# Batch-0 sink shares over all 128 partitions, constant rows as planned loads, loads without hold-back, and a new written-out order

## The chip, the cores and the metric

The kernel runs on one core of one Trainium2 chip. The metric is the device time of one execution in microseconds. It is compared as the median over runs. The profile shows five engines: PE (matmul; PEld is its weight load), DVE (vector), ACT (scalar), POOL (GpSimd) and SP, which here only issues DMAs. ACT and POOL issue DMAs as well, from the same instruction queue in which their other work stands.

## The reference

The program is an attention layer with sink tokens and a sliding window, followed by a ResMLP block. The sizes are 4 batches, 8 heads, 768 tokens, 64 values per head, so 512 values per token, and 2048 in the hidden layer.

```python
scores = scale * np.matmul(q, k.transpose(0, 1, 3, 2))
keep = (pos[None, :] < 4) | ((rel >= 0) & (rel < 128))      # 4 sink tokens, window of 128
a = softmax(np.where(keep, scores, -1e9))
x = np.matmul(a, v)  # -> [4, 768, 512]

a1 = alpha1 * x + beta1
tok = np.einsum('ts,bsd->btd', w_tok, a1)
u = x + lam * tok
a2 = alpha2 * u + beta2
ch = np.maximum(a2 @ w_ch1, 0.0) @ w_ch2
return u + lam * ch
```

## The kernel before

**Plan and order.** The kernel first lists tasks. Each task names its engine choices, what it needs and which buffers it uses (`add`). Four tables written out by hand then fix everything: `ORDER` is the sequence of the tasks, `ENGINES` the engine of each, `HOMES` the buffer of each tile, and `IDLES` where PE gets idle matmuls on a tile of zeros. `emit` walks through `ORDER`. Costs, due times (`lands`) and earliest times (`since`) that stand at the tasks do nothing when the kernel runs: they are what the tables were once planned from. Within one engine the instructions run in the order of the table.

**Batch 0.** Six q/k tiles of head pairs 1 to 3 are loaded by POOL with a cast to 16 bits (`n`); the two of head pair 0 are loaded by SP and cast on DVE. `trans` transposes them on PE (`tp`), and ACT or DVE copies them to `qkT`. `scores_by_pair` and `scores` make the scores of a block of 128 keys (S, in two PSUM buffers), and ACT takes the exponential (E). `sinks` does the same for the four sink tokens (`sk`, `es`): the score rows of two heads each lie at 32 partitions, so heads 0 to 3 (group G = 0) take partitions 0 to 63 and heads 4 to 7 (G = 1) partitions 64 to 127. `pv` multiplies E by v; from the third block of rows on it begins with the sink shares. DVE divides by the sum (`rec`, `x`), POOL multiplies by lam * alpha1 (`xh`).

**MLP.** `wtok` blocks are cast with their row sums, transposed and copied to `wtokT`. `tok` multiplies them with the xh of all six row blocks. `beta` and `ua` finish u on DVE, ACT or POOL cast it (`u16`), PE transposes it (`uTp`), and `mlp1` multiplies it with `w1f` (h). `w1f` arrives in four slices of 512 columns, loaded by POOL with a cast; h number fi needs slice fi // 4. Batch 0 ends with plain products (`mlp2`, ch). Batches 1 to 3 use half-size products of sums (`prod`, P). The attention of batch b + 1 is mixed into the MLP of batch b.

**Queues.** A DMA instruction waits in its engine's queue for what its buffer needs, and for the landing of an earlier DMA whose semaphore it uses again: SP and ACT share eight of these in turn, POOL has eight. Before the change, all twelve v loads of batch 0 (`load_v0`) are issued by SP. Three `gate` loads of a few bytes from w1f stand in SP's queue. Each waits until its w1f slice has landed, and the loads of batch 1 and of w2 are listed with such a gate's slice as a need.

**Constant rows.** lam, alpha1 and beta1 are each loaded to four partitions, and alpha2 and beta2 to `ab_row`, by five loads that ACT issues ahead of the planned order. `fold_rows` makes lam * alpha1 and lam * beta1 from them.

Of the kernel before, what the change touches and what calls it, by code (L numbers as in the profile page):

```python
# [77 lines left out]
def kernel(  # L78
# [17 lines left out]
    nc = tc.nc  # L96
# [45 lines left out]
        "nat": 8, "vnat": 4, "n16": 4, "qkT": 1, "E": 6, "es": 1, "x": 12, "xh": 6,  # L142
# [26 lines left out]
    nc.scalar.dma_start(ab_row[0:NC], moe_alpha2.rearrange("(c p) -> c p", p=P))  # L169
    nc.scalar.dma_start(ab_row[NC : 2 * NC], moe_beta2.rearrange("(c p) -> c p", p=P))  # L170
# [20 lines left out]
    for o_, src in ((lam_r, moe_lam), (la1_b, moe_alpha1), (lb1_b, moe_beta1)):  # L191
        nc.scalar.dma_start(
            o_.rearrange("(a i) d -> a i d", i=32)[:, 0, :], src.unsqueeze(0).to_broadcast([4, DM]))
# [4 lines left out]
    for r in range(NR):  # L198
# [13 lines left out]
    ROWS = 7000.0  # L212
# [4 lines left out]
        26, 6, 9, 7, 10, 5, 11, 8, 18, 15, 72, 19, 1, 12, 3, 0, 4, 2, 22, 14, 73, 74, 45, 48, 46,  # L217
        17, 39, 49, 47, 53, 13, 40, 50, 41, 90, 95, 43, 91, 51, 54, 103, 52, 16, 44, 61, 104, 42,
        96, 109, 100, 62, 107, 110, 63, 55, 28, 108, 92, 56, 101, 21, 68, 65, 59, 93, 20, 69, 97,
        102, 111, 94, 24, 98, 57, 60, 30, 112, 105, 23, 58, 99, 113, 128, 106, 114, 116, 25, 131,  # L220
        135, 78, 115, 64, 27, 138, 31, 32, 117, 132, 29, 129, 136, 33, 122, 66, 125, 34, 123, 137,
        119, 139, 126, 35, 79, 70, 120, 140, 124, 84, 71, 80, 133, 130, 141, 67, 146, 85, 134, 121,
        147, 144, 75, 118, 158, 86, 154, 148, 159, 145, 142, 87, 149, 150, 155, 160, 143, 76, 88,
        151, 156, 81, 77, 166, 152, 162, 167, 89, 127, 82, 163, 213, 83, 168, 209, 164, 165, 214,
        210, 153, 217, 179, 211, 178, 157, 197, 229, 36, 212, 215, 218, 185, 216, 226, 230, 219,
        176, 161, 177, 220, 169, 223, 222, 232, 225, 224, 221, 227, 237, 233, 279, 238, 234, 228,
        273, 280, 182, 171, 204, 291, 274, 175, 289, 292, 200, 231, 293, 290, 246, 294, 295, 199,
        384, 241, 248, 188, 186, 257, 296, 247, 172, 243, 277, 174, 181, 242, 259, 258, 187, 170,
        278, 267, 37, 260, 271, 358, 268, 198, 285, 349, 272, 381, 301, 286, 366, 351, 303, 302,
        189, 297, 378, 173, 304, 281, 180, 352, 203, 249, 190, 282, 298, 379, 250, 287, 380, 192,  # L230
        353, 385, 288, 206, 283, 386, 369, 375, 367, 265, 284, 368, 202, 370, 266, 363, 376, 371,
        253, 377, 201, 299, 254, 372, 364, 183, 382, 191, 300, 373, 615, 365, 275, 374, 383, 357,
        261, 276, 408, 262, 387, 263, 184, 409, 205, 195, 239, 411, 264, 410, 395, 269, 396, 240,
        397, 270, 196, 388, 614, 621, 235, 412, 400, 194, 244, 398, 236, 401, 255, 617, 251, 245,
        256, 389, 390, 399, 252, 311, 359, 207, 193, 391, 424, 616, 335, 425, 393, 341, 426, 392,
        336, 648, 427, 634, 413, 394, 312, 636, 414, 428, 419, 404, 420, 415, 360, 405, 313, 429,
        208, 422, 337, 416, 361, 441, 421, 622, 402, 314, 423, 442, 626, 403, 305, 638, 315, 406,
        430, 640, 316, 435, 431, 306, 641, 355, 436, 443, 619, 437, 338, 649, 618, 438, 362, 317,
        432, 637, 407, 307, 433, 345, 444, 339, 439, 635, 318, 445, 450, 434, 639, 644, 319, 451,
        628, 452, 620, 440, 308, 645, 340, 453, 417, 446, 323, 447, 418, 320, 309, 448, 324, 321,  # L240
        658, 322, 329, 449, 642, 659, 454, 325, 625, 643, 330, 646, 347, 455, 326, 623, 343, 647,
        464, 344, 456, 465, 348, 466, 460, 457, 467, 650, 327, 458, 331, 461, 629, 459, 472, 462,
        632, 463, 653, 356, 651, 656, 627, 332, 38, 654, 480, 333, 342, 624, 652, 473, 310, 476,
        468, 471, 470, 469, 481, 474, 488, 885, 477, 475, 482, 492, 655, 490, 493, 350, 483, 478,
        514, 491, 516, 489, 657, 479, 515, 660, 517, 630, 882, 665, 518, 663, 354, 328, 666, 502,
        880, 661, 664, 498, 879, 519, 508, 499, 346, 503, 678, 662, 512, 509, 679, 504, 513, 487,
        484, 671, 485, 676, 486, 506, 677, 877, 548, 505, 672, 680, 507, 526, 549, 546, 527, 631,
        334, 522, 674, 681, 528, 547, 907, 523, 534, 903, 529, 633, 682, 675, 878, 542, 683, 535,
        890, 689, 543, 550, 685, 684, 690, 510, 551, 494, 511, 673, 667, 544, 495, 668, 891, 496,
        686, 545, 901, 687, 669, 497, 693, 888, 688, 883, 530, 694, 670, 700, 531, 524, 897, 701,  # L250
        698, 500, 691, 525, 696, 699, 552, 501, 697, 704, 553, 558, 695, 705, 904, 692, 562, 559,
        706, 909, 887, 707, 563, 564, 898, 708, 702, 566, 565, 910, 715, 703, 567, 532, 716, 889,
        713, 533, 709, 714, 896, 520, 710, 556, 717, 521, 538, 557, 537, 540, 539, 536, 560, 541,
        899, 718, 921, 572, 922, 881, 711, 574, 884, 573, 576, 712, 561, 719, 902, 577, 575, 555,
        727, 720, 569, 908, 721, 580, 728, 578, 722, 581, 729, 554, 723, 905, 730, 568, 739, 724,
        579, 725, 592, 570, 911, 726, 582, 740, 593, 588, 912, 583, 595, 584, 571, 906, 743, 589,
        731, 585, 900, 590, 732, 605, 744, 587, 733, 596, 606, 734, 607, 611, 594, 597, 602, 745,
        612, 586, 613, 599, 895, 603, 591, 757, 765, 600, 758, 601, 759, 766, 741, 771, 760, 742,
        916, 772, 751, 917, 746, 773, 752, 913, 761, 919, 774, 886, 767, 918, 604, 762, 763, 598,
        768, 777, 764, 779, 920, 923, 780, 914, 755, 915, 778, 608, 756, 926, 930, 735, 609, 931,  # L260
        924, 927, 781, 736, 925, 775, 782, 737, 928, 753, 929, 893, 738, 934, 754, 892, 769, 935,
        932, 610, 941, 770, 819, 776, 942, 894, 939, 820, 821, 940, 937, 936, 823, 749, 822, 945,
        748, 824, 938, 747, 827, 933, 948, 950, 750, 952, 943, 951, 825, 953, 787, 828, 944, 807,
        788, 797, 826, 808, 949, 946, 829, 798, 801, 954, 830, 791, 802, 956, 947, 792, 783, 955,
        957, 963, 961, 784, 789, 958, 962, 811, 790, 964, 959, 785, 812, 965, 805, 786, 795, 806,
        960, 967, 796, 799, 793, 968, 966, 970, 972, 794, 813, 971, 969, 815, 973, 814, 809, 800,
        816, 803, 810, 974, 978, 804, 976, 979, 837, 975, 977, 835, 838, 980, 841, 836, 839, 842,
        818, 843, 840, 845, 981, 832, 982, 846, 817, 986, 844, 831, 990, 987, 983, 988, 847, 991,
        984, 851, 833, 992, 1002, 993, 834, 848, 855, 852, 985, 849, 1003, 859, 856, 1004, 989,
        1006, 850, 860, 1005, 853, 998, 1007, 1008, 868, 999, 857, 1009, 997, 865, 995, 858, 862,  # L270
        996, 869, 866, 1000, 874, 994, 854, 1001, 1016, 863, 875, 1040, 1017, 1038, 1041, 1032,
        1039, 871, 1020, 872, 1028, 1021, 1011, 1024, 1029, 1013, 1018, 1033, 1012, 1025, 1034,
        1019, 1036, 1010, 1035, 1042, 1037, 1076, 1043, 1070, 1077, 870, 1074, 1071, 1054, 1075,
        1022, 1055, 1060, 1023, 1048, 1061, 1058, 1049, 1066, 1059, 1014, 1044, 1015, 1067, 1072,
        1045, 1056, 1073, 1026, 1057, 1078, 1068, 1079, 1064, 1069, 1046, 1027, 1050, 1063, 1047,
        1052, 1082, 1053, 1051, 1084, 1083, 1062, 1065, 1030, 1085, 1080, 1101, 1031, 1081, 1091,
        1102, 1107, 1092, 1097, 1093, 1103, 864, 1108, 1105, 867, 1098, 1111, 1106, 1104, 1113,
        1112, 1089, 1114, 1115, 1086, 1116, 1090, 861, 1094, 1087, 1117, 1099, 1109, 1100, 1121,
        1095, 1110, 1125, 1118, 1122, 1124, 1134, 1126, 1123, 1128, 1135, 1127, 1119, 1136, 1088,
        1140, 1120, 873, 876, 1131, 1129, 1141, 1096, 1137, 1142, 1132, 1130, 1133, 1138, 1139,  # L280
    )
    ENGINES = (
# [22 lines left out]
        "1202002102135312330203"  # L305
    )
    IDLES = (
        (73, 0, 65), (46, 0, 12), (49, 1, 1), (90, 3, 10), (61, 3, 2), (109, 3, 3), (92, 3, 1),
        (166, 1, 4), (162, 0, 1),
    )  # L310
    W1_SINCE = 20000.0
# [3 lines left out]
    XB = 2  # L315
# [1007 lines left out]
```

The softmax here doesn't subtract the row's maximum and nothing guards it: scores larger than these inputs give would overflow.

## Time and profile before

| What | us |
|---|---|
| median of 3 runs | 258.96 (258.18 to 259.81) |
| profiled execution, span | 254.3 |
| PE busy / DVE / ACT / POOL | 245.6 / 190.7 / 133.2 / 103.2 |
| last PE matmul ends, last instruction of the chain on DVE | 250.06, 250.08 |
| first ACT copy | 8.13 |
| first scores of batch 0 on PE | 11.19 |
| first xh on POOL | 20.27 |
| idle matmuls on PE in the first 31 us | 99 in nine stretches |

The span runs from the first to the last instruction of the profiled execution. The median is of runs that are timed as a whole, so it is longer by what lies around the span. The granted TensorE clock is 0.997 of full speed. PE's busy time counts the idle matmuls too, and the ends of matmuls are modelled, so a busy PE in the first 31 us does not mean useful work. DMA is busy in the whole first half: its share in the 40 slices of the page is 0.6 or more up to slice 19. In what follows, L711 and the like are lines of the kernel before.

### The profile page before, as it was taken

To read this page: it belongs to the slowest core of one execution; us is meant where nothing else is said; L and a number is where in the kernel's file an instruction comes from. 1 tells how busy PE (TensorE), PEld (TensorE's weight loads), DVE (VectorE), ACT (ScalarE), POOL (GpSimd) and SP (SyncE) were. 2 spreads that over 40 slices of the span, in tenths; PEclk is the share of its full clock that TensorE was granted. 3 is DMA by queue.
4 is the path that set the end of the run, shared out by engine and by line. 5 is a ranking of instruction groups with operands and counts; after the bars stand their busy time and mean duration, and the time that the engine had idled before them with its cause. 6 is when DMAs were issued, how large, how long until landed. Compare 5 with 4: busy or idle time off the path is not lost.

```text
span 254.3 us, 5499 instructions
## 1 busy us (share of the span) xinstructions
PE 245.6 (97%) x2167; PEld 159.9 (63%) x2167; DVE 190.7 (75%) x402; ACT 133.2 (52%) x219; POOL 103.2 (41%) x124
## 2 busy tenths in 40 slices
PE   7799997999999999999999999999999999999993
PEld 7554644666555544566687686667667676667882
DVE  5688986767888874978879995578778983228892
ACT  2599913879977034787833434566660235543000
POOL 8318845876455527515782040065662120000010
PEclk9999999999999999999999999999999999999998
DMA  6999999899999999998484764520000140100327
GB/s 182 205 215 266 272 269 316 246 377 300 221 158 233 234 208 156 195 249 180 110 170 107 128 122 138 144 65 0 3 0 3 30 84 13 41 0 3 117 73 268
DMA packets 86129, 38.79 MB, mean 153 GB/s; under 512 B 73540, under 2 KB 80460, under 8 KB 86104
## 3 DMA queue, kind: packets, MB, share of 16 engines
q1 hardware_dynamic: 66576, 28.06, 47.3%
q10 hardware_dynamic: 15784, 7.11, 11.8%
q0 software_dynamic: 3744, 3.28, 8.0%
q8 instruction: 17, 0.28, 0.4%
q14 instruction: 8, 0.07, 0.1%
HBM read 29.91 MB, written 6.29 MB: 142 GB/s over the span
## 4 chain that ended last, share of the span: by engine, by line
PE 84%; DMA 11%; DVE 2%; POOL 1%; SPq 0%; issue 0%
PE h L929 32%; PE P L1046 22%; PE tok L849 9%; PE ch L1114 8%; DMA w1f<-in_moe_w_ch_dram 8%; PE pv L718 3%; PE S L617 3%; DMA nat<-in_k_dram 3%; PE tp L507 1%; POOL w1f L448 1%; PE tp L504 1%; DVE qkT L157 1%; DVE E L696 1%; PE pv L711 1%; PE pv L604 1%; PE idle L148 0%
## 5 line engine op out<-in xcount | busy, mean ns | idle before, releaser
L929 PE MATMUL h<-uT,w1f 128*128 128x384 f16 x512 | 89.8, 326 | 1.5 <-DMA w1f<-in_moe_w_ch_dram 1.5
L929 PEld LDWEIGHTS <-w1f 128*128 128x128 f16 x512 | 48.2, 98 | 32.7 <-DMA w1f<-in_moe_w_ch_dram 1.9
L935 ACT ACTIVATE hT<-h 128x384 f16<-128x384 f32 x77 | 37.0, 491 | 39.5 <-PE h L929 39.3
L937 DVE TENSOR_SCALAR hT<-h 128x384 f16<-128x384 f32 x51 | 27.8, 555 | 23.4 <-PE h L929 22.8
L1046 PEld LDWEIGHTS <-hT 128*128 128x128 f16 x408 | 39.5, 98 | 6.7 <-issue 0.2
L639 ACT ACTIVATE E<-S 128x1024 f16<-128x1024 f32 (+1 forms) x39 | 38.1, 1001 | 7.6 <-PE S L617 6.3
L762 POOL TENSOR_TENSOR tm<-x,la_b 128x512 f32<-128x512 f32 x18 | 24.3, 1353 | 24.2 <-DVE x L744 12.3
L849 PE MATMUL tok<-xh,wtokT 128*128 128x512 f16 x144 | 33.0, 379 | 0.0
L1059 DVE TENSOR_TENSOR x<-x,P 128x256 f32<-128x256 f32 x45 | 18.3, 419 | 11.3 <-PE P L1046 10.2
L1046 PE MATMUL P<-w2f,hT 128*128 128x256 f16 x216 | 26.5, 273 | 0.0
L849 PEld LDWEIGHTS <-wtokT 128*128 128x128 f16 x144 | 13.9, 98 | 15.0
L1114 PE MATMUL ch<-w2f,hT 128*128 128x512 f16 x96 | 23.2, 379 | 0.0
L1046 PE MATMUL P<-w2s,hT 128*128 128x256 f16 x192 | 23.1, 273 | 0.0
L1082 POOL TENSOR_TENSOR x<-x,pt 128x256 f32<-128x256 f32 x4 | 3.4, 854 | 47.5 <-DVE pt L1077 47.5
L155 ACT CAST u<-x 128x512 f16<-128x512 f32 x15 | 9.2, 615 | 24.9 <-DVE x L856 24.3
L744 DVE TENSOR_TENSOR x<-pv,rec 128x256 f32<-128x256 f32 x48 | 20.4, 425 | 1.7
L155 ACT CAST n<-nat 128x768 f16<-128x768 f32 x21 | 16.9, 828 | 8.9 <-DVE x L1125 6.4
L718 PEld LDWEIGHTS <-E 128*128 128x128 f16 x328 | 14.8, 98 | 5.1 <-issue 1.1
L856 DVE TENSOR_TENSOR x<-x,tok 128x512 f32<-128x512 f32 x24 | 16.0, 683 | 2.3 <-PE tok L849 2.3
L718 PE MATMUL pv<-vfs,E 128*128 128x65 f16 x328 | 17.7, 194 | 0.0
L579 POOL TENSOR_SCALAR_AFFINE_SELECT E<-E 128x512 f16<-128x512 f16 x12 | 7.5, 648 | 20.6 <-ACT E L639 20.6
L743 DVE RECIPROCAL rec<-pv 128x4 f32<-128x4 f32 x48 | 8.6, 179 | 7.2 <-PE pv L718 6.9
(134 smaller groups left out, 340.6 us busy)
## 6 DMA issues: line engine op xcount, KB each, us to landing
wst_w<-in_moe_w_ch_dram SPq DMA_DIRECT2D x8, 512.0 KB, 8.2
nat<-in_q_dram SPq DMA_DIRECT2D x10, 384.0 KB, 3.9
vnat<-in_v_dram SPq DMA_DIRECT2D x14, 256.0 KB, 5.7
nat<-in_k_dram SPq DMA_DIRECT2D x8, 384.0 KB, 7.2
out_dram<-x SPq DMA_DIRECT2D x11, 256.0 KB, 3.1
out_dram<-x ACTq DMA_DIRECT2D x10, 256.0 KB, 3.7
wtn<-in_moe_w_tok_dram SPq DMA_DIRECT2D x6, 384.0 KB, 4.1
w1f<-in_moe_w_ch_dram POOLq DMA_DIRECT2D x4, 512.0 KB, 15.4
```

Of the source, the lines that this page charges most:

```text
L155: nc.scalar.copy(o, i)
L639: nc.scalar.activation(eT.t, pS.t[:, :, 0 : n * w].rearrange("p e (i w) -> p e i w", i=n), AF.Exp, scale=scale)
L718: nc.tensor.matmul(po.t[:, hl, :], eT.t[:, e_, off + i, c : c + P], vf[j][:, h, :], start=(r < 2 and n == 0), stop=(n == len(parts) - 1 an ...
L744: nc.vector.tensor_mul(bx.t[:, 4 * G : 4 * G + 4, :], po.t[:, :, 0:D], rec.t.to_broadcast([P, 4, D]))
L762: engine[e].tensor_mul(bt.t, bx.t.rearrange("p h d -> p (h d)"), la1_b)
L849: nc.tensor.matmul(pt.t, wtokT[:, si, ti * P : (ti + 1) * P], hs[si].t, start=(si == 0), stop=(si == NR - 1))
L929: nc.tensor.matmul(ph.t, w1f[:, c, fi * P : (fi + 1) * P], bu.t[:, c, chk * NTOK : (chk + 1) * NTOK], start=(c == 0), stop=(c == NC - 1))
L935: nc.scalar.activation(bh.t[:, fi, :], ph.t, AF.Relu)
L937: nc.vector.tensor_scalar_max(bh.t[:, fi, :], ph.t, 0.0)
L1046: nc.tensor.matmul(pc.t, hh[:, nt * P : (nt + 1) * P], w(fi), start=(first and n_ == 0), stop=(n_ == HF - 1), skip_group_check=True)
L1059: nc.vector.tensor_add(row(bx)[:, cols], row(bx)[:, cols], pc.t)
L1114: nc.tensor.matmul(pc.t, bh.t[:, fi, nt * P : (nt + 1) * P], w2f[:, fi, :], start=(fi == 0), stop=(fi == NF - 1))
```

## The change

- The sink shares of batch 0 get one buffer for each group (`es`, two homes instead of one). The half of the partitions that belongs to the other group is set to zero by a new step on POOL or DVE, and `pv` multiplies over all 128 partitions instead of 64.
- The five row loads become planned tasks: lam and beta1 stay with ACT, alpha1, alpha2 and beta2 go to SP. The steps that use them list them as needs.
- v loads of batch 0 may be issued by ACT as well.
- The needs that held back loads of batch 1, 2 and 3, and of w2, and the transposes of batch 1, are taken away, and the loads list only their buffers. The three gate loads stay. The tasks for the loads of batch 1 and w2 are listed earlier (`load_rest`).
- ORDER, ENGINES, HOMES and IDLES are replaced as a whole.

```diff
-        "nat": 8, "vnat": 4, "n16": 4, "qkT": 1, "E": 6, "es": 1, "x": 12, "xh": 6,
+        "nat": 8, "vnat": 4, "n16": 4, "qkT": 1, "E": 6, "es": 2, "x": 12, "xh": 6,
...
-    nc.scalar.dma_start(ab_row[0:NC], moe_alpha2.rearrange("(c p) -> c p", p=P))
-    nc.scalar.dma_start(ab_row[NC : 2 * NC], moe_beta2.rearrange("(c p) -> c p", p=P))
...
-    for o_, src in ((lam_r, moe_lam), (la1_b, moe_alpha1), (lb1_b, moe_beta1)):
-        nc.scalar.dma_start(
-            o_.rearrange("(a i) d -> a i d", i=32)[:, 0, :], src.unsqueeze(0).to_broadcast([4, DM]))
...
     IDLES = (
-        (73, 0, 65), (46, 0, 12), (49, 1, 1), (90, 3, 10), (61, 3, 2), (109, 3, 3), (92, 3, 1),
-        (166, 1, 4), (162, 0, 1),
+        (54, 0, 45), (51, 1, 9), (109, 2, 24), (78, 0, 17), (58, 0, 5), (60, 2, 7),
     )
...
-    def load_qk(p, b, hp, t, wait=None):
+    def load_qk(p, b, hp, t):
...
-                p, {SP: 480, ACT: 550}, lambda e: queue[e].dma_start(bf.t, src), [wait], [bf], lands=(16, {(0, 0, 1): 85, (0, 1, 0): 140}.get((b, hp, t), 68)))
+                p, {SP: 480, ACT: 550}, lambda e: queue[e].dma_start(bf.t, src), uses=[bf], lands=(16, {(0, 0, 1): 85, (0, 1, 0): 140}.get((b, hp, t), 68)))
...
-            p, {SP: 520}, lambda e: nc.sync.dma_start(
+            p, {SP: 520, ACT: 560}, lambda e: queue[e].dma_start(
                 bf.t[:, sl], v[0, 4 * G : 4 * G + 4, r * P : (r + 1) * P, :].rearrange("h p d -> p h d")),
...
-        a = add(p, {PE: 336}, tr, [a, wait, done["iden"]], [bn, pt], mode="col" if direct else None)
+        a = add(p, {PE: 336}, tr, [a, done["iden"]], [bn, pt], mode="col" if direct else None)
...
-        if b not in es:
-            es[b] = Buf("es", None, None, f"es{b}")
-        o = qkT[b]
+        if b == 0:
+            es[b, Gs[0]] = Buf("es", None, None, f"es{b}_{Gs[0]}")
+        else:
+            es[b, 0] = es[b, 1] = Buf("es", None, None, f"es{b}")
+        o, eb = qkT[b], es[b, Gs[0]]
...
+        zero = None
+        if n == 1:
+            og = slice(64 - 64 * Gs[0], 128 - 64 * Gs[0])
+            zero = add(p - 1000, {DVE: 160, POOL: 300}, lambda e: engine[e].memset(eb.t[og], 0.0), uses=[eb], port=True)
...
-                g = slice(64 * G, 64 * G + 64) if b == 0 else slice(0, P)
                 nc.tensor.matmul(
-                    po.t, es[b].t[g, (r - 2) * P : (r - 1) * P], vs[g, 4 * G : 4 * G + 4, :],
+                    po.t, es[b, G].t[:, (r - 2) * P : (r - 1) * P], vs[:, 4 * G : 4 * G + 4, :],
                     start=True, stop=False)
...
+        rows = {}
+        for name, o_, src in (("lam", lam_r, moe_lam), ("a1", la1_b, moe_alpha1), ("b1", lb1_b, moe_beta1)):
+            rows[name] = done["row", name] = add(-990, {SP: 500, ACT: 510}, lambda e, o_=o_, src=src: queue[e].dma_start(
+                o_.rearrange("(a i) d -> a i d", i=32)[:, 0, :], src.unsqueeze(0).to_broadcast([4, DM])),
+                lands=(2, 45))
...
+    def load_rest():
+        for i, (hp, t) in enumerate(QK_ORDER):
+            load_qk(t0 + 100 + i, 1, hp, t)
...
```

The new order, where it differs in the first 50 us, engine by engine:

- SP: k and q of head pair 0, a w_tok block, a v tile, the alpha1 row, five v tiles, a w_tok block, two v tiles, then beta2, w_tok, v, alpha2, v and two w_tok blocks; three q/k tiles of batch 1; the first gate; the other loads.
- ACT: the rows of lam and beta1; copies, a w_tok cast and exponentials of head pairs 0 and 1; a v load; five exponentials and a copy; a v load; an exponential; a w_tok load; the rest of group 1.
- POOL: zeroing of one `es` half, the first q load of head pair 1, the identity, the masks, the other five q/k loads, two v casts with lam * alpha1 between them, a third v cast, the first two w1f slices, all twelve xh, the third slice, a u cast, the fourth slice.
- PE: all six tok products ahead of the first uTp (before: five of them), three transposes of batch 1 ahead of the first h, and h in another order.

## The prediction

> **What bounds the kernel now.** I read the chain of waits first, then the timeline of PE, then ACT, POOL and the SP queue in the first 45 us. The chain (start, length, engine, what):
>
> ```profile
> 21.01 2.22 POOL w1f L448 x3
> 23.23 20.17 DMA w1f<-in_moe_w_ch_dram
> ...
> 43.45 2.12 PE h L929 x12
> ...
> 233.45 16.61 PE P L1046 x152
> ```
>
> From 43.45 to 250.06 the chain has PE alone: 206.6 us without a gap above 0.1 us. Its work is the same in both kernels, so the time is decided by when that solid stretch begins. The timeline of PE before it (start, length, operation; in brackets the idle time and its releaser):
>
> ```profile
> 31.39 6.64 PE L849 MATMUL tok<-xh,wtokT 128*128 128x512 f16 x30
> ...
> 39.83 2.11 PE L929 MATMUL h<-uT,w1f 128*128 128x384 f16 x12
> ...
> 43.45 2.12 PE L929 MATMUL h<-uT,w1f 128*128 128x384 f16 x12 [1.50 <-DMA w1f<-in_moe_w_ch_dram]
> ```
>
> PE is solid from 31.39 on but for 1.50 us, in which it waits for the fourth slice of w1f. So before, h begins in effect at 39.83 + 1.50 = 41.33. What sets 31.39? The timeline of ACT:
>
> ```profile
> 23.31 1.02 ACT L639 ACTIVATE E<-S 128x1024 f16<-128x1024 f32 x1
> 24.23 0.83 ACT L814 ACTIVATE wt<-wtn 128x768 f16<-128x768 f32 x1
> ...
> 28.86 1.05 ACT L639 ACTIVATE E<-S 128x1024 f16<-128x1024 f32 x1
> ...
> 30.59 0.83 ACT L155 COPY wtokT<-wT 128x768 f16<-128x768 f16 x1
> ```
>
> ACT has only 0.4 us of idle time between 16.3 and 31.4, and the copy that ends at 31.42 releases tok. ACT bounds the head of the kernel. POOL and SP in the same time, and then how long the v loads of batch 0 take:
>
> ```profile
> 2.24 11.45 SPq L424 DMA_DIRECT2D v<-in_v_dram  x7
> ...
> 13.73 2.71 SPq L435 DMA_DIRECT2D wtn<-in_moe_w_tok_dram  x1
> ...
> 16.49 1.53 SPq L424 DMA_DIRECT2D v<-in_v_dram  x3
> ...
> 20.96 3.05 POOL L448 DMA_DIRECT2D w1f<-in_moe_w_ch_dram  x4
> ...
> DMA to landing us min/median/max: 4.8/9.0/10.2
> ```
>
> SP needs 11.45 us to issue seven v loads. In the program each hardware load waits, in its issuing engine's queue, for the load eight before it. Today that wait stands in SP's queue, where nobody computes.
>
> **The new wait.** In the new order three loads of batch 0 stand in ACT's queue: a v tile after the exponentials of head pair 1, a second v tile, and a w_tok block. The first waits for the landing of the v load that is 14th in SP's queue (v0_0, rows 4), eighth among the v loads. Queued behind it on ACT are five exponentials of group 0, the copy of the last k transposes and all of group 1; PE's scores wait for the two S buffers that these free, DVE and POOL for pv.
>
> When does ACT get there? Its k tile of head pair 1 is now POOL's second casting load, behind the identity (0.2 + 0.3 us in its rows) and five mask steps (1.4), so it is issued near 4.3, where the first is issued at 1.3 as before and takes 0.9. The n loads took 6.7 to 8.3 us to land, so it lands at 11 to 12.6. Transposes, copy and exponentials of the pair (some 4 us) bring ACT to its load at 15 to 16. That the tiles of head pair 0 are now first in SP's queue moves the first scores ahead of 11.19, but the pair behind them does not follow.
>
> When is it released? The eighth v load was issued at 16.49 today, behind the same three big tiles, seven v tiles and one w_tok block; the smallest landing time gives 21.3. If SP were not held up in issuing (the previous issue began at 13.73) it would be 18.5. I take 20.5, nearer to the row in the same place of the queue. So ACT stands still for some 5 us.
>
> What follows on ACT up to the last exponential of group 1, by start to start in the timeline: five of 512 columns at 0.5 = 2.5, seven of 1024 at 0.92 = 6.4, a copy 0.7, two v casts 1.3, one w_tok cast 0.8: 11.7 us. The issue itself is 0.4. Waits for scores were 0.4 in all in this stretch today; with PE held back at the S buffers they can be 2; I take 1.5. Sum: 20.5 + 0.4 + 11.7 + 1.5 = 34.1, and 0.7 for the transposes and the pv behind: tok begins at 34.8 instead of 31.39.
>
> POOL is a second path to the same point. The v tile loaded by ACT lands 4.8 later, at 25.7; its cast (0.8) now stands ahead of the first two w1f issues (1.6) and of all twelve xh products (0.70 to 0.78 each). Nine of them are needed for the first tok: 25.7 + 0.8 + 1.6 + 6.6 = 34.7. The two paths agree.
>
> From tok to h, PE now has 36 tok matmuls at 0.22 (7.9), two w_tok transposes (0.7), two u transposes (0.7) and three transposes of batch 1 moved ahead (1.0; taken off the later stretch): 10.2. First h: 45.0. Against before: 45.0 - 1.0 - 41.33 = +2.7.
>
> **The w1f slices.** Slices 0 and 1 are issued near 27, and with landings of 9.6 to 14.2 (the median of the four was 15.4) they are there by 41. Slice 2 follows the twelfth xh (37), slice 3 the u cast behind tok, three beta rows and a w_tok cast on DVE (41). The lowest landing in the trace is 9.6, the highest 20.2 with four in flight. At 9.6 they land at 46.6 and 50.6; h wants them at 47.0 and 49.6, so the last is 1.0 late. With fewer in flight it can be less: I add 0.5 and keep 0 and 11 (at 20.2) as ends. The 1.50 us stall of today is already out of the sum.
>
> **The other edits.** The sink shares: eight pv of batch 0 go from 64 to 128 rows. Timeline of PE, a pair in each form:
>
> ```profile
> 22.51 0.28 PE L711 MATMUL pv<-vs,es 64*128 64x260 f16 x1
> 22.73 0.41 PE L718 MATMUL pv<-vfs,E 128*128 128x65 f16 x8
> ...
> 70.30 0.27 PE L711 MATMUL pv<-vs,es 128*128 128x260 f16 x1
> 70.41 0.41 PE L718 MATMUL pv<-vfs,E 128*128 128x65 f16 x8
> ```
>
> The next matmul starts 0.22 us after the half-height one and 0.11 after the full one: 8 x 0.11 = 0.9 us of PE. I count it at nothing, for PE fills gaps with idle matmuls there (nine stretches, 99 in all) and ACT is late; without that cover it would be a gain of 0.9. The two zeroings cost 0.2 to 0.5 on POOL, ahead of its first load, and 0.1 to 0.2 on DVE, both before ACT's wait: nothing. The constant rows leave ACT's first 4 us, when it computes nothing (its first copy is at 8.13), and two small ones stand in SP's queue; la is wanted by the first xh, long after: nothing, 0.5 if SP is late by one issue each. The freed loads: three q/k tiles of batch 1 (1.2 MB) now go ahead of the gate in SP's queue, where two w2 blocks and lam_b (1.3 MB) went at 26 to 27; the rest still stand behind that gate. Nothing, since DMA is full either way (share 0.97 to 1.24 from 20 to 46 us); one tile's landing of 5.5 us is the most that could reach PE. Solid stretch and tail: another order of equal work, more v loads in ACT's queue (bounds -0.5 to +2): 0.
>
> Sum: +2.7 + 0.5 = +3.2 on a span of 254.3 and the 4.7 us between span and median: 258.96 + 3.2 = 262.1.
>
> The Trainium skill, "DMA: Bandwidth & Descriptors", section "Issuing engines are not separate DMA queues", speaks against the move of loads to ACT: it says that this saves only the sequencer's issue time. No row here shows a v load issued from ACT; by the rule the transfers gain nothing, and the sum stays as it is.
>
> The same page, "Anatomy of one DMA", puts a DMA at 2.0 us plus its bytes at 436 GB/s, an estimate of 2.3 us for a v tile. The landings of 4.8 to 10.2 us differ from it; by the page's figure ACT would be released at 18.8 and the sum would be 260.4.
>
> **Rivals.** First, the wait is short: SP issues earlier, as ACT has taken loads off it, and ACT goes on at 17. Then the v tile from ACT lands in the crowd, in the median 9.0 us: at 26, and POOL's path (9.0 us of work behind it) puts tok at 35.0 again; in the least, 4.8, at 30.8. The middle, 32.9, is +0.8, or 259.8. The 11.45 us of SP's issue row speak against it.
>
> Second, faster: the early scores pull everything ahead and ACT's v load lands within 4.8 us of 15.5. Then casts, w1f and nine xh end at 29.3, tok begins at 29, h at 39.2: 39.2 - 1.0 - 41.33 = -3.1, 255.8. It decides if the eighth v load has landed when ACT reaches its own. For it: the stall of 1.50 is gone. Against: 16.49 + 4.8.
>
> Third, worse: the last w1f slice, issued late and alone with batch 1's loads, takes 14 us and more. It lands at 55, PE waits 5: 267. For it: landings of 15.4 and 20.2; against: these had four in flight.
>
> **How the numbers follow.** Forecast 0.50 (260.5 to 264.5), short wait 0.22, faster 0.15, late slice 0.13. A difference of 1%, 2.6 us, is about what a measurement of this kernel can tell from none. Slower than 261.55: 0.40 of the forecast, the late slice, 0.03 of the short wait: 0.56. Faster than 256.4: 0.13. The rest, 0.31, lies between. The range of 257.5 to 266 leaves out most of the faster case and half of the late slice. The forecast's own range is 260.5 to 264.5.
>
> **What would show it.** ACT idle for 3 us or more between 15 and 21 before an exponential, released by a v load; tok starting near 35; the first two w1f issues at 26 to 28; first h near 45; PE solid behind it for about 206 us. I am wrong if ACT has no such gap, or if tok starts before 31.4, or if PE has new gaps behind 50 us.

## The result and the profile after

The kernel after takes 272.37 us in the median (271.93 to 272.92, 4 runs), the kernel before 258.57 in the same comparison (255.47 to 259.81). The ratio is 1.0584, with a 95% interval of 1.0504 to 1.0665. The prediction was 262.1, with a range up to 266.0: slower as forecast, but by 13.8 us instead of 3.2.

The profiled execution has a span of 271.2 us against 254.3. I split these 16.9 us at the first h, with the stall of 1.50 us that before has behind it counted to the head:

| Stretch | before | after | difference |
|---|---|---|---|
| start to first h | 41.33 | 51.77 | +10.44 |
| first h to the end of the last P | 208.73 (to 250.06) | 216.07 (to 267.84) | +7.34 |
| tail | 4.24 | 3.36 | -0.88 |

In the later runs, which list time and span of the same execution, the two lie 1.7 to 2.4 us apart, and not the 4.7 us of the prediction. So the profiled execution of before, at 256 to 257, was one of its shorter ones, and the medians differ by less than the spans. Some executions of a kernel are disturbed (over 1.5% above its fastest, most of them at a lower clock): medians and ratios below are of the others, and for two kernels (before_three_u and new_head_old_rest) too few others were left for a ratio, so that the range is given and the profile is of a disturbed one.

The timeline of ACT (start, length, operation; in brackets the idle time and its releaser) shows the predicted wait, and then a second one:

```profile
19.30 0.41 ACTq L422 DMA_DIRECT2D v<-in_v_dram  x1
19.76 0.60 ACT L643 ACTIVATE E<-S 128x512 f16<-128x512 f32 x1 [4.34 <-DMA v<-in_v_dram]
...
24.96 0.39 ACTq L422 DMA_DIRECT2D v<-in_v_dram  x1
...
35.03 0.84 ACT L155 CAST vfs<-v 128x768 f16<-128x768 f32 x1 [3.34 <-DMA v<-in_v_dram]
```

ACT stands still for 4.34 us until it has issued its first v tile. At 24.96 it issues the second, and the cast of that same tile starts 10.07 us later, after ACT has stood still for 3.34 us. The chain of waits has the tile by name, and the SP queue shows what was issued just ahead of it, three tiles of batch 1 of 384 KB each:

```profile
24.96 10.05 DMA v<-in_v_dram
```

```profile
23.42 0.38 SPq L395 DMA_DIRECT2D nat<-in_q_dram  x1
23.90 0.93 SPq L395 DMA_DIRECT2D nat<-in_k_dram  x2
38.11 0.73 SPq L453 DMA_DIRECT2D gates<-w1f  x1
```

PE answers with two gaps. tok begins 8.4 us later than before, and h 10.4 us later than it did in effect:

```profile
20.41 1.01 PE L616 MATMUL S<-biasn,iden 128*128 128x512 f16 x2 [3.97 <-ACT E L643]
...
35.92 0.54 PE L721 MATMUL pv<-vfs,E 128*128 128x65 f16 x7 [3.15 <-ACT vfs L155]
...
39.82 2.93 PE L852 MATMUL tok<-xh,wtokT 128*128 128x512 f16 x8
...
51.77 2.76 PE L932 MATMUL h<-uT,w1f 128*128 128x384 f16 x16
```

Behind the first h, where before has no gap above 0.1 us but the stall of 1.50, PE waits for DVE. These are the five longest of its waits from 60 to 265 us (total, times, longest):

```profile
PE P L1049 <- DVE x L747: 1.5, 1, 1.5
PE h L932 <- DVE x L859: 1.4, 1, 1.4
PE P L1049 <- DVE x L1062: 0.8, 1, 0.8
PE pv L721 <- DVE x L747: 0.7, 1, 0.7
PE P L1049 <- DVE vs L575: 0.5, 1, 0.5
```

All eight add up to 5.7 of the 7.34 us. The rest, and the 1.0 us that the three transposes moved ahead of h should have saved, lies in small delays between matmuls that no run here takes apart.

DVE's busy time went from 190.7 to 207.2 us, in 421 instructions instead of 402. Part of this is dearer instructions, not more of them: the six sums hS took 6.4 us before and take 8.6. Here they are in before and then in after (min/median/max in ns, start of the first and the last):

```profile
L987 DVE TENSOR_TENSOR hS<-hT,hT x6: 944/953/1768, 132.9 to 232.2; 128x1536 f16<-128x1536 f16 x6
```

```profile
L990 DVE TENSOR_TENSOR hS<-hT,hT x6: 948/1429/2026, 147.5 to 247.6; 128x1536 f16<-128x1536 f16 x6
```

### The profile page after: what moved, and what is told of

Read it like the earlier page. It is cut to its first block, busy times and chain, and to the rows that moved or that the text cites. A ratio compares the mean times of both kernels' runs of the same rounds, so it can differ in the third digit from the quotient of the medians.

```text
span 271.2 us, 5544 instructions
## 1 busy us (share of the span) xinstructions
PE 252.3 (93%) x2175; PEld 163.7 (60%) x2175; DVE 207.2 (76%) x421; ACT 125.5 (46%) x201; POOL 105.3 (39%) x129
## 4 chain that ended last, share of the span: by engine, by line
PE 56%; DVE 24%; DMA 10%; issue 4%; POOL 2%; ACT 1%; SPq 1%; ACTq 0%; DVEq 0%; POOLq 0%
PE h L932 22%; PE P L1049 18%; PE tok L852 7%; DMA v<-in_v_dram 6%; DVE w2f L834 4%; PE pv L721 3%; DVE hT L940 2%; DMA lam_r<-in_moe_lam_dram 2%; DVE x L777 2%; DVE E L658 2%; DVE hS L990 2%; PE ch L1117 2%; POOL tm L765 1%; DVE x L747 1%; PE S L621 1%
## 5 line engine op out<-in xcount | busy, mean ns | idle before, releaser
L932 PE MATMUL h<-uT,w1f 128*128 128x384 f16 x512 | 90.8, 326 | 2.0 <-DVE x L859 1.4
L938 ACT ACTIVATE hT<-h 128x384 f16<-128x384 f32 x68 | 32.3, 490 | 43.9 <-PE h L932 43.3
L940 DVE TENSOR_SCALAR hT<-h 128x384 f16<-128x384 f32 x60 | 32.4, 553 | 18.3 <-PE h L932 17.2
L852 PE MATMUL tok<-xh,wtokT 128*128 128x512 f16 x144 | 34.0, 387 | 0.3 <-DVE x L1128 0.3
L583 POOL TENSOR_SCALAR_AFFINE_SELECT E<-E 128x512 f16<-128x512 f16 x20 | 13.8, 713 | 32.2 <-ACT E L643 32.2
L721 PE MATMUL pv<-vfs,E 128*128 128x65 f16 x328 | 18.6, 198 | 4.1 <-ACT vfs L155 3.2
L721 PEld LDWEIGHTS <-E 128*128 128x128 f16 x328 | 16.3, 101 | 9.5 <-issue 4.3
L1088 POOL TENSOR_TENSOR x<-x,pt 128x512 f32<-128x512 f32 x4 | 5.9, 1475 | 41.6 <-issue 32.4
L747 DVE TENSOR_TENSOR x<-pv,rec 128x256 f32<-128x256 f32 x48 | 20.4, 425 | 1.7
L157 POOL CAST u<-x 128x512 f16<-128x512 f32 x9 | 6.0, 662 | 31.4 <-DVE x L859 27.6
L155 ACT CAST n<-nat 128x768 f16<-128x768 f32 x17 | 13.6, 831 | 4.2 <-DMA qkT<-n 3.2
```

The lines of the kernel that those rows point to most:

```text
L155: nc.scalar.copy(o, i)
L721: nc.tensor.matmul(po.t[:, hl, :], eT.t[:, e_, off + i, c : c + P], vf[j][:, h, :], start=(r < 2 and n == 0), stop=(n == len(parts) - 1 an ...
L747: nc.vector.tensor_mul(bx.t[:, 4 * G : 4 * G + 4, :], po.t[:, :, 0:D], rec.t.to_broadcast([P, 4, D]))
L852: nc.tensor.matmul(pt.t, wtokT[:, si, ti * P : (ti + 1) * P], hs[si].t, start=(si == 0), stop=(si == NR - 1))
L932: nc.tensor.matmul(ph.t, w1f[:, c, fi * P : (fi + 1) * P], bu.t[:, c, chk * NTOK : (chk + 1) * NTOK], start=(c == 0), stop=(c == NC - 1))
L938: nc.scalar.activation(bh.t[:, fi, :], ph.t, AF.Relu)
```

## The experiments

The lines of the experiments' kernels lie a few numbers higher than those of after. "First h" is its start in the profile; each ratio is against before measured beside it, in one of four groups of runs (its medians there were 257.0, 257.2, 258.9 and 256.3). As before itself moves by 2.6 us between these groups, a difference of that size between kernels of different groups is read from the profiles, not from the medians.

### Which part: the parts, the head, the rest

**old_order_new_parts**: ORDER, ENGINES and IDLES of before, with the seven new tasks put in (rows on ACT at the start, zeroings on POOL). The second sink buffer left no room for the fourth u buffer.

> The new tasks (sinks over 128 rows, two zeroings, five row loads) in the old written-out order and on the old engines. Theory A (all of the loss comes from the new order, the parts cost nothing): 258.6 +- 1.3 us. Rival B (the parts themselves cost): 262 or more, with first h later than 39.8. If the shorter pv gap (8 x 0.11 us) pays: 257.7.

Measured: 258.55 us, ratio 1.0073 (1.0029 to 1.0117). Tok began at 30.54, h at 38.98. So the parts are not what costs 5.8%. The profile has a stall of 3.12 us for the fourth w1f slice (before 1.50) and a gap of 1.88 us at 111, in front of a pv that waits for ACT.

**before_three_u**: the kernel before, with three u buffers. A control for this gap.

> The kernel before with three instead of four buffers for u, nothing else: a control for the new parts in the old order, which had to give up that buffer and measured 0.7% above before. Theory A (the buffer costs it, not the parts): the gap of 1.9 us in front of a pv near 111 is there, 0.5 to 1% above before. Rival B (the parts cost it): as before, within 0.3%, no such gap.

Measured: 257.43 to 264.29 us, without a ratio. The gap is there without any new part, as the list of PE's waits from 60 to 262 us shows:

```profile
PE pv L726 <- ACT hT L943: 1.9, 1, 1.9
```

So the gap comes from the missing buffer. Whether the parts by themselves cost or save a few tenths stays open: it is below what these runs can tell.

**old_head_new_rest** and **new_head_old_rest**: both kernels take the new parts. The first has the old order up to the first h and the new one behind it, the second the reverse.

> Up to the first h the old order, behind it the new order with its engines (eight instructions stand a few places earlier, since one w2 load has to wait for a buffer). The profile of after puts the loss at 10.4 us ahead of the first h and 7.4 us behind it. Theory A (the part behind h loses by itself, because DVE is full from 60 to 83 us with casts of w2 that POOL did before): 258.6 + 7.4 = 266. Rival B (it loses only because the head brings its loads late): 258.6 to 260.

Measured: 269.55 us from two executions, ratio 1.0501 (1.0428 to 1.0574). First h at 47.44: ahead of it PE waits 3.57 us for a cast of a batch 1 tile that the old head loads late, a fault of the splice. Behind it the waits of after come back one by one, of the same size: 1.5, 1.4, 0.8, 0.5, 0.3 and 0.2 us; those of 0.7 and 0.3 us ahead of 100 us do not. From first h to the last P it takes 216.2 us, as in after (216.07). So the rest loses by itself.

> The new order up to the first h, the old one behind it. Theory A (head and rest lose each by itself): 258.6 + 10.4 = 269. Rival B (the late head drags the rest, whatever its order): 273 or more. First h stays near 51.8 in both, as nothing ahead of it is changed.

Measured: 267.3 to 274.63 us, without a ratio. First h at 48.29, though it was expected near 51.8, and a wait of 4.89 us at 59.95, where the splice holds up the second half of uT. From 80 us on PE has no gap. The time decides nothing here; the profile says the same as that of the kernel above, from the other side.

### The head

**v_loads_on_sp**: the change in the table of engines is this, and nothing else (the table holds digits; here they stand with the names of their tasks).

```diff
-  load_v0(1, 2): ACT    load_v0(1, 5): ACT    load_wtok(3): ACT
+  load_v0(1, 2): SP     load_v0(1, 5): SP     load_wtok(3): SP
```

> After, with its three loads in ACT's queue (two v tiles, one w_tok block) issued by SP from the same places of the order. Theory A (ACT stands at these loads): the idle time of 4.3 us in front of the exponential at 19.8 is gone and tok starts 4 us earlier, near 36: 268; if the second stall (3.3 us in front of the v cast at 35.0) falls with it, 265. Rival B (ACT would wait for the same v tiles anyhow): 271 or more, with the idle time moved to a v cast or to scores.

Measured: 263.76 us, ratio 1.0313 (1.0237 to 1.0388): 8.6 us less than after by the medians, 2.7% by the ratios. ACT has no idle time above 0.7 us from 14 to 29 us, and PE:

```profile
29.52 1.89 PE L856 MATMUL tok<-xh,wtokT 128*128 128x512 f16 x8
...
41.34 2.76 PE L936 MATMUL h<-uT,w1f 128*128 128x384 f16 x16
```

First h comes 10.43 us earlier than in after. That is all of the head's 10.44. SP issues the last v tile at 19.3, where ACT issued its second at 24.96. The tok matmuls start even earlier than before (31.39): the early scores of the new order do pay, once no load stands among the exponentials. But from tok to h it takes 11.82 us (before 8.44 and the stall), so that h is where before had it in effect, at 41.33.

**first_v_on_sp**: only the first v tile goes to SP.

> After, with only the first of ACT's three loads (the v tile behind head pair 1) issued by SP; the second v tile and the w_tok block stay on ACT. Theory A (ACT's wait at the first load starts the whole delay): the gap of 4.3 us is gone, the second stall shrinks too, since ACT issues the second tile earlier; first h near 43 to 46 instead of 51.8, 264 to 267 us. Rival B (it is the second tile, 10.05 us from issue to landing, that decides): first h above 48, 269 or more.

Measured: 269.94 us, ratio 1.0503 (1.0422 to 1.0585), first h at 50.26. ACT issues the second tile at 22.50, 2.5 us earlier than in after, but it lands only 1.4 us earlier, at 33.58 instead of 35.01, and ACT stands 5.50 us at its cast. Rival B: the second tile alone is enough to keep most of the delay.

**second_v_on_sp**: the second v tile and the w_tok block go to SP, the first v tile stays on ACT.

> After, with the second v tile and the w_tok block on SP and the first v tile left on ACT. Theory A (the first wait of ACT costs its 4.3 us whatever follows, the second tile the rest): the gap of 4 us stays, the second stall is gone; first h near 46, 267 to 268. Rival B (the second tile is the whole loss): 264 to 265. Rival C (nothing without the first): 270 or more.

Measured: 270.78 us (270.38 to 273.12), ratio 1.0557 (1.0461 to 1.0652), first h at 48.75. The second stall is gone, the wait for the first load is now 4.86 us. By the time it is rival C, by the start of h between A and C: the profile has h 3.0 us earlier, the median is 1.6 us less. Neither of these two edits takes away one wait and leaves the rest alone. In first_v_on_sp the second tile's own landing got longer (11.08 us instead of 10.05). In second_v_on_sp the turn of the eight semaphores falls differently, and ACT's first load waits for a w_tok block that lands at 20.75; in after it waited for a v load that landed at 19.28. So the first h comes 1.5 and 3.0 us earlier, which do not add up to 10.43.

**nat_behind_gate**: ACT's loads stay; the three tiles of batch 1 move.

```diff
-  SP: ... load_wtok(5), load_qk(1,2,0), load_qk(1,2,1), load_qk(1,3,1), gate(1), ...
+  SP: ... load_wtok(5), gate(1), load_qk(1,2,0), load_qk(1,2,1), load_qk(1,3,1), ...
```

> After, with the three freed q and k tiles of batch 1 (1.2 MB) moved back behind the gate on the second w1f slice; ACT's loads stay. Theory A (the second v tile takes 10.05 us because it stands behind these three): it lands in 5 to 6 us, the second stall (3.3 us in front of the v cast) is gone: 3 to 5 us faster than after, 267 to 269. Rival B (it is slow for another reason, or the first stall hides it): 271 to 273.

Measured: 268.27 us, ratio 1.0440 (1.0345 to 1.0534), 4.1 us less than after; first h at 46.84. The second v tile is issued at 25.61, and ACT comes to its cast without a wait:

```profile
32.66 0.83 ACT L155 CAST vfs<-v 128x768 f16<-128x768 f32 x1
```

So the second stall is made by the three freed tiles, which are transferred together with the v tile (DMA share 0.97 and 1.16 from 25 to 35 us in after). They need not stand ahead of it: in first_v_on_sp one of them was issued before the v tile, at 21.57, and two behind it, at 22.58 and 23.52, and it took 11.08 us all the same. The first wait of ACT is still there (3.87 us).

**both_loads**: the two edits together.

> Both of the load edits together: three loads on SP and the three freed tiles of batch 1 behind the gate. Each alone gave -8.6 and -4.1 us. Theory A (both remove the same wait of ACT for the second v tile, so they do not add): 262.5 to 264.5. Rival B (they add): 259 to 260.

Measured: 267.03 us, first h at 42.89: by its median worse than either theory. The ratio, 1.0310 (1.0245 to 1.0374), is that of v_loads_on_sp, but against a slower before; the span is 3.8 us longer than there. The tiles of batch 1 now come too late:

```profile
38.56 0.83 ACT L155 CAST n<-nat 128x768 f16<-128x768 f32 x1 [5.00 <-DMA nat<-in_k_dram]
```

This cast stands in ACT's queue in front of the casts of u. With the v loads on SP, freeing the three tiles does no harm, and by the profile it helps.

**idle_in_stalls**: two stretches of idle matmuls on PE, 62 in front of the score task at 20.4 us and 48 in front of the pv task at 32.5 (the first number is the task's place in the list).

```diff
+    (113, 3, 62), (165, 0, 48),
```

> After, with 62 and 48 idle matmuls put on PE where it stands still in front of 20.4 and 32.5 us, so that it is busy in both stalls; no wait is changed. Theory A (the granted clock of 0.50 behind the two stalls costs time of its own): clock 1.00 from 20 to 42, the first eight tok matmuls 1.9 us instead of 2.9, first h near 50, 1.5 to 2.5 us faster, 270 to 271. Rival B (ACT and POOL set the pace there, the clock costs nothing): first h at 51.8 and 272.4.

Measured: 270.08 us, ratio 1.0501 (1.0408 to 1.0593), whose interval overlaps that of after. In after the granted clock halves behind each stall; these are rows of PE in windows of 5 us (window, length, PE busy, clock, DMA share, GB/s):

```profile
20.00:25.00 5.00, 4.59 (x48) 0.51 0.64 212
25.00:30.00 5.00, 5.00 (x61) 1.00 0.97 256
30.00:35.00 5.00, 2.77 (x47) 1.00 1.16 223
35.00:40.00 5.00, 4.08 (x45) 0.51 0.29 58
```

With the idle matmuls the first and the last of these have a clock of 1.00 (0.92 and 0.74 between them), and the first eight tok matmuls take 1.89 us instead of 2.93. But tok starts at 39.87 (39.82), the last six tok wait 0.75 us for DVE, and h starts at 51.60 (51.77). So the first h speaks for rival B: the clock is a result of the stalls here, and costs h 0.2 us. The median, 2.3 us less than after, is where theory A had it, and stays unexplained: it is of another group of runs, and the profiled execution's span is 0.8 us less. The edit also made a new wait of PE for DVE, of 2.12 us, in front of 29.34.

### The rest

**sp_w2_on_pool** (on top of v_loads_on_sp):

```diff
-  cast_w2, six of 16: DVE
+  cast_w2, six of 16: POOL
```

> The kernel with the three loads on SP (263.8 us), and the six casts of w2 that went from POOL to DVE back on POOL. Theory A (these six, 0.86 us each on DVE, fill DVE from 50 to 75 us and so delay PE): 2 to 4 us faster, 260 to 262, the gap of PE in front of pv at 72.7 gone. Rival B (the gaps behind 95 us, which are other DVE work, carry most of it): 263 to 264.

Measured: 266.13 us, ratio 1.0330 (1.0240 to 1.0419). No gain; the gap in front of pv, at 72.7 in v_loads_on_sp and at 75.2 here, grows from 0.68 to 2.17 us. Theory A falls: fewer instructions on DVE, more on POOL, and DVE is no earlier.

**sp_old_engines** (on top of v_loads_on_sp): behind the first h, 139 entries of the table of engines are those of before.

> The kernel with the three loads on SP (263.8 us); for every computing instruction behind the first h that changed its engine in the edit (139 of them, among ACT, DVE and POOL) the old engine is put back; the new order and the engines of the loads stay. Theory A (the new engines overload DVE, 207 us of busy time against 191): DVE's busy time falls to some 192, the gaps of PE behind h (6.6 us) shrink below 2, 257 to 259. Rival B (the written-out order makes the gaps): 262 or more.

Measured: 266.38 us, ratio 1.0287 (1.0215 to 1.0359). DVE has 403 instructions again (402 in before), but takes 197.3 us for them instead of 190.7, and PE has more gaps, not fewer. So the count of instructions on DVE is not the cause.

**sp_head_old_rest** (v_loads_on_sp up to the first tok, then the old order on the old engines, three u buffers):

> The new order with the three loads on SP up to the first tok matmul, behind it the old order on its old engines (three instead of four buffers for u). Theory A (the loss behind h belongs to the new order and engines, and the new head is no loss once ACT issues no loads): tok at 29.5, no gap of PE behind 60 us, 256 to 258.5, level with before or a little faster. Rival B (the new head leaves its late loads to any rest): 261 or more, with gaps from 45 to 80.

Measured: 263.66 us, ratio 1.0185 (1.0107 to 1.0264). That is rival B's time, and tok starts at 33.54, not at 29.5: in the old order it waits for the last w_tok blocks, which ACT casts up to 33.1. Two gaps are left behind the first h at 41.98: 2.67 us for a w1f slice, and the 2.2 us of the missing u buffer. Less these, first h to the last P takes 210.4 us. None of the waits of the new order is there, and in this theory A is right.

**sp_sum_later** (on top of v_loads_on_sp): in DVE's queue

```diff
-  ..., w2 sum (1.37 us), x <- x + tok, ...
+  ..., x <- x + tok, w2 sum, ...
```

> The kernel with the three loads on SP, with one sum of two w2 blocks on DVE (1.37 us beside POOL's like sum, 0.42 in the old order) put behind the tok addition that it stood in front of. Theory A (each gap behind h is one local place of DVE's queue): the gap of 1.41 us in front of h of batch 1 is gone, 1.4 us less in the span, 262.4. Rival B (DVE is full there, the gap only moves): span as before, 261.6, the gap a few us later.

Measured: 263.35 us, ratio 1.0177 (1.0101 to 1.0252). The median is level with that of v_loads_on_sp (263.76); the ratio is lower because before was 1.9 us slower beside it. The gap of 1.41 us is gone, and two of 0.49 and 0.50 stand behind it, for vs and x. First h to the last P: 216.8 us, as in v_loads_on_sp (216.9). Nearer to B: DVE is late there whatever comes first.

**sp_pool_short** (on top of v_loads_on_sp): DVE keeps its work and order, POOL's in-place work is cut down.

```diff
-   keep(ev[:, :, 0:P], 0, 1, -1)
-   if w > P:
-       keep(ev[:, :, P:w], -1, -1, 1)
+   keep(ev[:, 0:1, 0:P], 0, 1, -1)
...
+   if e == POOL and n_ == 1:
+       ab = [x_[:, :, 0:8] for x_ in ab]
...
+   c = slice(0, 8 if e == POOL else HD)
...
```

> The kernel with the three loads on SP; POOL's in-place work behind h is cut to a few columns: its window masks (first column of heads only), its in-place sum of w2 blocks, its additions of a product to x (8 columns). So the output is another; order, engines and DVE's work stay. Theory A (DVE is slowed by POOL working beside it): the DVE sum near 106 takes 0.42 instead of 1.37 and the gap of 1.41 in front of h of batch 1 shrinks to 0.5 or less, the gap of 0.79 at 217 (beside POOL's additions) is gone, while the gaps at 142 and 197 (beside POOL's tm and xh, untouched) stay at 0.45 and 1.47; 2 to 3 us less, 261 to 262. Rival B (the places in DVE's queue alone): all gaps stay within 0.2 us, 263 to 264.

Measured: 260.06 us, ratio 1.0134 (1.0093 to 1.0174), against 1.0313 for the kernel that it is made from. The same w2 sum on DVE and the same h behind it, first in v_loads_on_sp:

```profile
106.32 1.37 DVE L968 TENSOR_TENSOR w2f<-w2f 128x512 f16<-128x512 f16 x1
...
106.25 1.16 POOL L968 TENSOR_TENSOR w2f<-w2f 128x512 f16<-128x512 f16 x1
...
108.34 2.31 PE L936 MATMUL h<-uT,w1f 128*128 128x384 f16 x12 [1.41 <-DVE x L863]
```

then in sp_pool_short:

```profile
104.07 0.43 DVE L968 TENSOR_TENSOR w2f<-w2f 128x512 f16<-128x512 f16 x1
...
104.00 0.22 POOL L968 TENSOR_TENSOR w2f<-w2f 128x16 f16<-128x16 f16 x1
...
105.15 2.31 PE L934 MATMUL h<-uT,w1f 128*128 128x384 f16 x12 [0.46 <-DVE x L861]
```

The same instruction takes 0.43 us instead of 1.37 when POOL's like sum beside it is short, and the gap behind it shrinks from 1.41 to 0.46. The gap of 0.79 at 217, beside POOL's additions, is gone. Of the gaps beside tm and xh, which were left alone, one stays at 0.45 and the other goes from 1.47 to 0.76. First h to the last P takes 212.6 us instead of 216.9. Theory A holds, for 4.2 us of the excess. Part of the gain may be work that is missing on POOL itself; the instruction's own time is the direct evidence. 3.9 us more than in before remain, of which 2.9 are waits; no run takes away the POOL work that was left alone.

The traces of before and after show the same without any edit. Together they have 38 sums of these two kinds on DVE, of w2 blocks and hS. 23 begin while POOL is idle, and 3 when POOL's running instruction has at most 0.15 us left: all take 0.41 to 0.42 us (w2) or 0.94 to 0.96 (hS). The other 12 begin while a POOL instruction (tm, xh, a cast, a w2 product or sum) has 0.55 us or more left, and each is longer by what is left, less some 0.14 us. There are four of these in before and eight in after, and they cost 2.8 and 6.3 us more than the same sums beside an idle POOL.

**new_head_old_parts**: a try at a kernel that beats both: the new head with no load on ACT, all four w1f slices together, sinks over 64 rows, four u buffers, the old order behind the first tok.

> The kernel before (sinks over 64 rows, rows issued by ACT at the start, four u buffers) with the new order up to the first tok matmul, ACT's three loads on SP and all four w1f slices issued together, and the old order behind it. Theory A (the new head without loads on ACT is as fast as the old one, the old rest has no gaps): 256 to 259, level with before, a gain only where the w1f stall of 1.5 us falls away. Rival B (its w_tok loads come late): tok near 33.5 and 260 to 262.

Measured: 257.81 us, ratio 1.0021 (0.9978 to 1.0064): level with before. PE has no wait above 0.15 us from the first h, at 43.22, to the end; the stall for w1f is gone, and the later start of h gives it back. No version here beats before.

## Why the prediction was wrong

**ACT's wait: right.** Forecast: reached at 15 to 16, released at 20.5, some 5 us. Measured: idle from 15.4 to 19.76, 4.34 us, released by a v load. That the time of release came so close is luck: two errors cancel. SP issued the eighth v load at 11.99 and not at 13.73 to 16.49, and it took 7.3 us to land and not 4.8. The estimate of 2.3 us by the Trainium skill, "DMA: Bandwidth & Descriptors", section "Anatomy of one DMA", was further off; that section is about DMAs issued by GpSimd, and this load is SP's.

**"Two v casts 1.3": the first step that failed.** ACT's 11.7 us after the release were priced as work alone, with 1.5 us for scores as the only wait. The second of these casts needs the v tile that ACT itself issues at 24.96, which landed 10.05 us later; ACT stood 3.34 us more, and PE 3.15. I had the two paths, of ACT and of POOL, from the first tile only, and asked of the second load no more than the time to issue it. tok came at 39.82 instead of 34.8. Of these 5.0 us the stall is 3.34; more waiting for scores (2.4 us instead of 1.5), dearer work (12.6 instead of 11.7) and a later tok behind the last exponential (1.7 instead of 0.7) make up the rest, less 1.1 for the earlier release.

**"The freed loads: nothing, since DMA is full either way": failed with it.** I asked what the three tiles do to the gate and to PE, and bounded them at 5.5. They were issued at 23.42 to 24.83, right ahead of the second v tile, and nat_behind_gate shows that they held it up: without them ACT has no second stall, and the first h comes 4.9 us earlier. That the DMA is full either way does not make a load harmless: it makes it matter what else is issued in the same microseconds.

**POOL's path: harmless in after.** The first w1f slices were issued at 24.31, not at 26 to 28, as the third tile's cast began at 23.54 and not at 25.7. In second_v_on_sp, which has only the wait that the prediction had priced, this path is as forecast: the tile lands at 25.78 and the first w1f slice is issued at 26.60. Even there tok begins only at 36.91 (forecast 34.8). **w1f + 0.5: nothing came of it**: no h waited for w1f. The third and fourth slice were issued at 41.43 and 45.32, later than forecast, but h was later still.

**From tok to h, 10.2: measured 11.95.** The terms of this sum add up to 10.3. The first eight tok ran at half the clock (2.93 us instead of 1.89), and the three transposes of batch 1, with waits among them, took 1.7 us instead of 1.0. The clock is not the whole of it: in v_loads_on_sp and idle_in_stalls those eight take 1.89 us, and tok to h still 11.82 and 11.73, with waits of 0.82 and 0.75 us among the tok.

**Sinks, zeroings, rows at nothing: not refuted.** In after the matmul behind a full-height sink pv starts 0.11 to 0.12 us after it (25.83 to 25.95), as read from before. The old order with all of them is within 0.3 to 1.2% of before, with a gap in it that a buffer explains.

**"Solid stretch and tail 0, bounds -0.5 to +2": the second step that failed.** The stretch took 7.34 us more, though 1.0 us of transposes had left it. I took "another order of equal work" for equal time, and looked only at loads in ACT's queue. The profile of before had the evidence: hS took 0.95 us in the median and 1.77 at most, and the w2 sums 0.41 to 1.20. The same instruction was dearer in some places, and a new order moves the places. Here the Trainium skill, "SBUF — State Buffer", section "Who interferes with whom", would have named what to look for: DVE and GpSimd share a pair of ports, and a DVE instruction with two inputs in SBUF contends with a GpSimd one that reads SBUF. The rows agree: beside POOL the sum took 1.37 us instead of 0.43, while DVE's instructions that read PSUM (hT, 0.55) took the same in both kernels. The runs show the price at the kernel too: with POOL's in-place work cut down, the stretch of v_loads_on_sp fell from 216.9 us to 212.6. What made the 3.9 us that are left above before stays open.

**The rivals.** None happened. The sign that I had named for being wrong did: new gaps of PE behind 50 us. The rule that speaks against loads on ACT (the Trainium skill, "DMA: Bandwidth & Descriptors", section "Issuing engines are not separate DMA queues") agrees with the runs: three loads back on SP, 8.6 us less. But it speaks of what is gained, and the loss was in ACT's own work.

**A reading of before that was off.** tok starts at 31.39, 0.03 us before the end of the copy that the prediction names as its releaser. That copy cannot have released it. The sum uses only the start of tok.

## What to carry to other kernels

When a load moves into the queue of an engine that computes, price two waits for it: the one until it may be issued, and the one of the work on that engine that needs what it brings, by what else is issued around it. An order of equal work is not equal time: look in the profile for one instruction whose shortest and longest times lie far apart, find what runs beside it, and see where the new order puts the two together. An edit that takes one wait away can move or lengthen another: undo the waits one by one and together, and look in each profile at what is waited for, before saying what each is worth.

## What the runs showed of the hardware

- Issuing a DMA earlier into a full stage gained less than it looked: the second v tile took 10.05 us from 24.96 and 11.08 us from 22.50, so 2.46 us at the issue were 1.43 us at the landing. The v tiles that SP issued in the same two kernels took 7.8 and 9.4 us in the median.
- Gaps of 3.15 and 3.97 us on PE were followed by half the granted clock (0.51 from 35 to 40 and from 20 to 25 us); the stall of 1.50 us in before left it at 1.00. The length of a gap alone does not decide: behind one of 1.40 us at 109.37 in both_loads the clock fell (0.66 from 110 to 115), behind one of 2.67 us at 44.09 in sp_head_old_rest it did not (1.00 from 45 to 55). Idle matmuls kept it up in the two stalls, and moved the first h by only 0.2 us.
- DVE's hS (two inputs of 128x1536 in 16 bits) took 0.95 us in the median of before, and 1.91 and 2.02 in one pair of v_loads_on_sp, beside POOL's multiplications. In before and after a sum on DVE was slowed only when POOL's instruction was already running, and then by about what that had left; where POOL began later, hS kept its 0.95 us (at 187.83 in before, at 147.52 in after). Only the effect of POOL's in-place work was tested by a run of its own.
